# A rebuilt opening for a fused convolution and two-matmul kernel: shorter band construction, w_in in column halves, another channel order

## Chip, cores, metric

One core of a Trainium2 chip; the batches of runs went to different chips, so each run is compared with executions of the kernel before in its own rounds. The metric is the device time of one execution in microseconds (us); executions of one kernel in the same rounds lay within 0.4% of each other. In the traces PE is TensorE and PEld its weight loads, DVE is VectorE, ACT ScalarE, POOL GpSimd, SP the engine whose queue issues most of the DMAs; PSUM is the memory that matmuls write.

## The reference

x is 8 x 4096 x 192, weight 8 heads x 7 taps, w_in 192 x 2048, w_out 2048 x 192, all fp32. (Shortened:)

```python
def _attn_ref(x, weight):                       # causal convolution, one set of taps a head of 24 channels
    w = softmax(weight, axis=-1)
    x_pad = concatenate([zeros((B, 6, D)), x], axis=1)
    x_unf = x_pad[:, idx, :].reshape(B, S, K, H, group)
    return einsum('hk,bskhg->bshg', w, x_unf).reshape(B, S, D)

def _moe_ref(x, w_in, w_out):
    h = x @ w_in
    return (h * cos(h)) @ w_out
```

## The kernel before: the parts that matter

32,768 tokens are cut into 64 tiles of 512, two tiles to a unit. For each half unit the convolution is 12 matmuls on half of PE's rows (64 of 128 tokens) with band matrices as weights. Its output is transposed by DMA and feeds the first matmul (`mm1`, 192 channels as three chunks k of 64, each on an upper and a lower row half at once); then cosine on ScalarE, product on VectorE, and the second matmul (`mm2_step`).

```python
w_src = moe_w_in.rearrange("(h k r) (t f) -> k t h r f", h=H, r=R, t=2)   # channel = (head, k, r), R = 8
for k in range(NC):
    for t in range(2):
        nc.sync.dma_start(out=w_f[64 * t : 64 * t + 64, k, :, :]..., in_=w_src[k, t])     # 8 x 8 x 1024

def conv_view(ps, n):                            # where a convolution matmul writes in PSUM
    return ps[:, :, 0 : n * 2 * G].rearrange("p b (n k i r) -> p b i n k r", n=n, k=NC, i=2)

def conv_mm(u, c, pv, i, rows, prev, n0, n1, **flags):
    h = 4 * c + i
    return nc.tensor.matmul(out=pv[:, i // 2, i % 2],
        lhsT=band[rows, h, 128 if prev else 0 : 256 if prev else 128],
        rhs=bf[u][rows, n0 + 1 - prev : n1 + 1 - prev, h * G : (h + 1) * G].rearrange("p n (k r) -> p n k r", k=NC), ...)

def conv_part(u, c, ...):                        # one half unit; up = rows 0-63, lo = rows 64-127
    mm(0, up, start=True); mm(2, lo, start=True); m = mm(1, up)
    mm(2, lo, 1); mm(3, lo)
    turn.mark(m, mm(3, lo, 1))                   # ... cut
    turn.wait(mm(0, lo)); mm(0, lo, 1); mm(1, lo)
    turn.wait(mm(2, up)); mm(1, lo, 1, stop=True); mm(3, up, stop=True)
```

## Time and profile before

| | before |
|---|---|
| time, median of 4 runs | 755.75 us (755.13 to 756.02) |
| start of tile 0, 1, 2 (first mm1 matmul) | 19.6, 34.4, 52.08 us |
| from tile start to tile start, tiles 2 to 60 | 11.12 us |
| the same without convolution (last tiles) | 10.57 us |

The time of such a program is two numbers: when tile 2 starts, and the period of a tile times some 60. Two lines are needed besides those that the prediction shows. A second steady tile in the windows view (columns: start:end, length, then busy time and count on PE, weight load, DVE, ACT, POOL, then clock, DMA share, GB/s), and the group of the convolution's matmuls in the middle of the run, from 100 to 700 us (columns: out and in, shapes, count, busy us, mean ns of one, idle before):

```profile
63.16:74.28 11.12, 11.12 (x194) 9.96 (x191) 9.43 (x9) 9.66 (x13) 0.00 (x0) 1.00 0.40 123
```

```profile
L168 PE MATMUL h<-x_bf,band 64*128 64x192 bf16 x648 | 61.6, 243 | 0.0
```

The first is the regular period, 11.12; PE is busy throughout. In the second, 243 ns is how long one matmul is in the pipe. It is not its cost: successive convolution matmuls on one row half start 82 ns apart in the trace (108.408, 108.490, 108.573 us).

### The profile page before, as it was taken

How to read it: one execution, taken by the hardware profiler on the slowest of the kernel's cores; microseconds unless marked ns; L12 is line 12 of the kernel's file. 1: busy time of each engine (PE TensorE's matmuls, PEld its weight loads, DVE VectorE, ACT ScalarE, POOL GpSimd, SP SyncE). 2: the span in 40 equal slices, each digit the busy share in tenths (PEclk: the TensorE clock that was granted, in tenths of full speed). 3: DMA queues.
4: the chain of work that ended last, by engine and by line, in shares of the span. 5: the costliest groups of instructions: out<-in, count | busy, mean ns of one | idle time of the engine just before them, and what ended most of it. 6: DMA issues, size and time to landing. Idle time of an engine off the chain costs nothing.

```text
span 753.7 us, 26680 instructions
## 1 busy us (share of the span) xinstructions
PE 724.6 (96%) x12060; PEld 646.8 (86%) x12060; DVE 616.5 (82%) x533; ACT 624.4 (83%) x778; POOL 110.0 (15%) x112
## 2 busy tenths in 40 slices
PE   1699999999999999999999999999999999999997
PEld 1378999999999999999999999999999999999876
DVE  5658888888888888888888888888888888888893
ACT  3668888888888888888888888888888888888883
POOL 4310111110111110011111011111101111101000
PEclk9989999999999999999999999999999999999999
DMA  7434334334535424433432442442454543243301
GB/s 203 113 86 127 85 108 127 94 99 127 116 77 127 127 77 116 127 90 103 128 105 88 127 120 73 127 127 74 119 128 89 104 127 107 86 128 85 82 27 64
DMA packets 167633, 79.99 MB, mean 106 GB/s; under 512 B 99552, under 2 KB 167136, under 8 KB 167520
## 3 DMA queue, kind: packets, MB, share of 16 engines
q1 hardware_dynamic: 167376, 78.26, 39.1%
q8 instruction: 94, 1.54, 0.8%
q14 instruction: 19, 0.16, 0.1%
q10 hardware_dynamic: 144, 0.03, 0.0%
HBM read 28.34 MB, written 25.17 MB: 71 GB/s over the span
## 4 chain that ended last, share of the span: by engine, by line
PE 95%; POOL 1%; issue 1%; DVE 1%; ACT 1%; DMA 1%; POOLq 0%; SPq 0%
PE h L264 46%; PE o_ps L290 45%; PE h L168 3%; DMA w_bc<-in_weight_dram 1%; POOL x_bf L157 0%; POOL wo L360 0%; DVE strip L123 0%; DVE band L125 0%; ACT o_sb L302 0%; ACT cs L270 0%; DVE prod L121 0%; POOL band L125 0%; ACT w L250 0%; POOL ct L218 0%; ACT ct L182 0%
## 5 line engine op out<-in xcount | busy, mean ns | idle before, releaser
L274 DVE TENSOR_TENSOR g<-h,cs 128x1024 bf16<-128x1024 f32 x512 | 605.5, 1221 | 115.8 <-ACT cs L270 108.9
L270 ACT ACTIVATE cs<-h 128x1024 bf16<-128x1024 f32 x512 | 511.4, 1025 | 78.9 <-PE h L264 74.3
L290 PE MATMUL o_ps<-wo,g 64*128 64x192 bf16 x8192 | 452.5, 243 | 1.2 <-ACT o_sb L302 1.2
L290 PEld LDWEIGHTS <-g 64*128 64x128 bf16 x8192 | 419.8, 94 | 35.8 <-SPq L138 1.8
L264 PE MATMUL h<-cT,w 64*128 64x512 bf16 x3072 | 439.1, 379 | 2.9 <-ACT ct L182 1.3
L264 PEld LDWEIGHTS <-w 64*128 64x128 bf16 x3072 | 234.1, 94 | 37.9 <-issue 4.1
L218 POOL COPY ct<-ct 128x1536 bf16<-128x1536 bf16 (+1 forms) x32 | 46.4, 1449 | 580.9 <-ACT ct L182 580.9
L168 PE MATMUL h<-x_bf,band 64*128 64x192 bf16 (+2 forms) x784 | 74.7, 247 | 19.7 <-DVE band L125 11.4
L168 PEld LDWEIGHTS <-band 64*128 64x128 bf16 (+1 forms) x784 | 56.2, 96 | 27.6 <-DVE band L125 11.4
L182 ACT CAST ct<-h 128x384 bf16<-128x384 f32 (+1 forms) x128 | 54.4, 477 | 23.9 <-PE h L168 19.2
L302 ACT COPY o_sb<-o_ps 128x384 f32<-128x384 f32 x128 | 61.3, 479 | 10.1 <-PE o_ps L290 8.2
L157 POOL CAST x_bf<-x_f 128x1536 bf16<-128x1536 f32 (+1 forms) x32 | 46.3, 1448 | 3.1 <-DMA x_f<-in_x_dram 3.1
L156 POOL COPY x_bf<-x_bf 128x192 bf16<-128x192 bf16 x24 | 8.4, 349 | 0.0
L180 ACT CAST ct<-h 128x384 bf16<-128x384 f32 x2 | 1.0, 480 | 6.8 <-PE h L168 6.8
L121 POOL TENSOR_TENSOR prod<-mask,wn 128x1064 f32<-128x1064 f32 x1 | 3.4, 3387 | 4.6 <-DVE wn L116 4.6
L180 DVE CAST ct<-h 128x384 bf16<-128x384 f32 x2 | 1.1, 558 | 3.1 <-ACT ct L180 3.1
L109 ACT ACTIVATE wexp<-wexp 128x56 f32<-128x56 f32 x1 | 0.2, 249 | 3.4 <-DVE wexp L108 3.4
L360 POOL CAST wo<-wo_f 128x1536 bf16<-128x1536 f32 x2 | 2.9, 1469 | 0.0
L243 PE MATMUL h<-ident,ct 128*128 128x128 bf16 x12 | 1.5, 312 | 1.2 <-DVE ct L180 1.2
L123 DVE TENSOR_REDUCE strip<-prod 128x152 f32<-128x1064 f32 x2 | 2.5, 1260 | 0.1
L243 PEld LDWEIGHTS <-ct 128*128 128x128 bf16 x12 | 1.2, 144 | 1.4 <-DVE ct L180 1.4
L88 ACT ACT_TABLE_LOAD x1 | 1.3, 1283 | 1.2 <-PEq L394 1.2
(29 smaller groups left out, 18.3 us busy)
## 6 DMA issues: line engine op xcount, KB each, us to landing
out_dram<-o_sb SPq DMA_DIRECT2D x64, 384.0 KB, 2.8
x_f<-in_x_dram SPq DMA_DIRECT2D x31, 768.0 KB, 12.9
w_f<-in_moe_w_in_dram SPq DMA_DIRECT2D x6, 256.0 KB
wo_f<-in_moe_w_out_dram SPq DMA_DIRECT2D x1, 1536.0 KB
x_f<-in_x_dram SPq DMA_DIRECT2D x2, 384.0 KB, 8.9
cT<-ct SPq DMA_TRANSPOSE x32
w_bc<-in_weight_dram ACTq DMA_DIRECT2D x1, 28.0 KB, 4.8
```

Source lines behind the costliest of these rows:

```text
L121: eng.tensor_tensor(out=prod[:, hs], in0=mask.rearrange("p (o e) k -> p o e k", o=1).to_broadcast([128, 4, E, K]), in1=wn[:, hs].to_broadc ...
L156: nc.gpsimd.tensor_copy(out=bf[u][:, 0, :], in_=bf[u - 1][:, UB, :])
L157: copy(out=bf[u][:, n0 + 1 : n1 + 1, :], in_=x_tiles[u][:, n0:n1, :])
L168: return nc.tensor.matmul(out=pv[:, i // 2, i % 2], lhsT=band[rows, h, 128 if prev else 0 : 256 if prev else 128], rhs=bf[u][rows, n0 + 1 ...
L182: copies[b](o[:, :, 0, :], i[:, :, 0, :])
L218: nc.gpsimd.tensor_copy(out=ct[:, n0:n1, :, 1, :], in_=ct[:, n0:n1, :, 0, :])
L264: nc.tensor.matmul(out=h[:, i, :], lhsT=w[rows, k, j, :], rhs=c[rows, n0 : n0 + NB, k, :], start=(k == 0), stop=(k == NC - 1))
L270: nc.scalar.activation(out=cs, in_=h, func=AF.Sin, bias=math.pi / 2.0, scale=1.0)
L274: nc.vector.tensor_tensor(out=g_tiles[t][:, 2 * j : 2 * j + 2, :], in0=h, in1=cs, op=ALU.mult)
L290: m = nc.tensor.matmul(out=o_ps[tt, b][:, si * D : (si + 1) * D], lhsT=g_tiles[tt][rows, f, s * 128 : (s + 1) * 128], rhs=wo[rows, f // 2, ...
L302: nc.scalar.copy(o_sb[t][:, 2 * b : 2 * b + 2, :].rearrange("p s d -> p (s d)"), o_ps.pop((t, b))[:, 0 : 2 * D])
L360: nc.gpsimd.tensor_copy(out=wo[:, :, i, :], in_=wo_f[:, i])
```

## The change

Its intent is to start tile 0 and tile 1 sooner. The taps come as one row and are broadcast by a PE matmul; the bands are built from bf16 products of 8 taps (one of them zero) and a tree of adds on DVE alone; 19 matmuls on zeros keep PE's clock up; w_in comes in two column halves, so that tile 0 can begin on the first; unit 0's whole convolution runs ahead of tile 0. To load a column half in one DMA with 128 rows, the order of the channels within a chunk is changed too, from (head, k, r) to (row, k).

```diff
-    w_bc = consts.tile([128, H, K], FP32)       # taps to 128 rows by DMA
+    w_row = consts.tile([1, H * K], FP32)       # one row, then a PE matmul with ones
...
-    w_src = moe_w_in.rearrange("(h k r) (t f) -> k t h r f", h=H, r=R, t=2)
-    for k in range(NC):
-        for t in range(2):
-            nc.sync.dma_start(out=w_f[64 * t : 64 * t + 64, k, :, :]..., in_=w_src[k, t])
-    load_unit(0, NB, UB)
+    w_src = moe_w_in.rearrange("(m k) (t f) -> k t m f", k=NC, t=2)
+    HP = NP // 2
+    for q in range(2):
+        for k in range(NC):
+            nc.sync.dma_start(out=w_f[:, k, q * HP : (q + 1) * HP, :]...,
+                              in_=w_src[k, :, :, q * HP * 128 : (q + 1) * HP * 128])
...
+    keep_warm(3) ... keep_warm(16)              # 512-column matmuls on zeros
...
-    for eng, hs in ((nc.vector, slice(0, 4)), (nc.gpsimd, slice(4, 8))):
-        eng.tensor_tensor(out=prod[:, hs], ...)               # fp32, 7 taps
-        nc.vector.tensor_reduce(out=strip[:, hs], ...)
+    for hs in (slice(0, 4), slice(4, 8)):
+        nc.vector.tensor_tensor(out=prod[:, hs], ...)         # bf16, 8 taps
+        for m in (4, 2):
+            nc.vector.tensor_tensor(out=prod[:, hs, :, 0:m], in0=prod[:, hs, :, 0:m], in1=prod[:, hs, :, m : 2 * m], op=ALU.add)
         for q in range(4):
-            eng.tensor_copy(out=band[...], in_=strip[...])
+            nc.vector.tensor_tensor(out=band[...], in0=prod[p, hs, :, 0], in1=prod[p, hs, :, 1], op=ALU.add)
...
-        return ps[:, :, 0 : n * 2 * G].rearrange("p b (n k i r) -> p b i n k r", n=n, k=NC, i=2)
+        return ps[:, :, 0 : n * 2 * G].rearrange("p b (n k i r) -> p b i n r k", n=n, k=NC, i=2)
...
-            rhs=bf[u][...].rearrange("p n (k r) -> p n k r", k=NC),
+            rhs=bf[u][...].rearrange("p n (r k) -> p n r k", k=NC),
...
-    PE_FIRST = "h0 a1 h1 a2 b1 h2 b2 h3 | h4 h5 d1 h6 d2 c1 h7 c2 x"
+    PE_FIRST = ["h0 h1 h2 h3 h4 h5 h6 d1 h7 d2 c1 c2 |", "h0 m8 h1 m8 h2 h3 m16 | h4 c1 h5 m8 c2 h6 m12 h7 m12"]
```

(Cut: the order of casts and of w_out's loads, the masks in bf16, the generators for the opening.)

More of the change, by code (lines that the diff above doesn't have):

```diff
@@ L58 @@
     ctx.enter_context(tc.manual_schedule())
-    w_bc = consts.tile([128, H, K], FP32)
-    nc.scalar.dma_start(out=w_bc, in_=bass.AP(tensor=weight.tensor, offset=weight.offset, ap=[[0, 128], [K, H], [1, K]]))
+    w_row = consts.tile([1, H * K], FP32)
+    nc.scalar.dma_start(out=w_row, in_=weight.rearrange("(o h) k -> o (h k)", o=1))
     x_tiles = {}
@@ L72 @@
     load_unit(0, 0, NB)
+    load_unit(0, NB, UB)
     w_f = consts.tile([128, NC, NP, 128], FP32)
-    w_src = moe_w_in.rearrange("(h k r) (t f) -> k t h r f", h=H, r=R, t=2)
-    for k in range(NC):
-        for t in range(2):
-            nc.sync.dma_start(out=w_f[64 * t : 64 * t + 64, k, :, :].rearrange("p j f -> p (j f)"), in_=w_src[k, t])
-    load_unit(0, NB, UB)
+    w_src = moe_w_in.rearrange("(m k) (t f) -> k t m f", k=NC, t=2)
+    HP = NP // 2
+    for q in range(2):
+        for k in range(NC):
+            nc.sync.dma_start(out=w_f[:, k, q * HP : (q + 1) * HP, :].rearrange("p j f -> p (j f)"),
+                              in_=w_src[k, :, :, q * HP * 128 : (q + 1) * HP * 128])
@@ L80 @@
     load_unit(1)
-    wo_f = consts.tile([128, 2, NP, D], FP32)
-    nc.sync.dma_start(out=wo_f, in_=moe_w_out.rearrange("(i j p) d -> p i j d", i=2, p=128))
-    one = consts.tile([128, 1], FP32)
+    wo_f = consts.tile([128, NP, 2, D], FP32)
+    wo_src = moe_w_out.rearrange("(i j p) d -> p j i d", i=2, p=128)
+    one = consts.tile([128, 128], FP32)
     nc.vector.memset(one, 1.0)
-    scrap = consts.tile([128, 1], FP32)
-    nc.scalar.activation(out=scrap, in_=one, func=AF.Exp)
-    E = 32 + K - 1
@@ L92, with keep_warm @@
-    mask = consts.tile([128, E, K], FP32)
+    zero = consts.tile([128, T], BF16)
+    nc.vector.memset(zero, 0.0)
+    idle = o_pools[0].tile([128, T], FP32, name="o_ps0")
+    def keep_warm(n):
+        for _ in range(n):
+            nc.tensor.matmul(out=idle, lhsT=zero[:, 0:128], rhs=zero, start=True, stop=True)
+    scrap = consts.tile([128, 1], FP32)
+    nc.scalar.activation(out=scrap, in_=one[:, 0:1], func=AF.Exp)
+    keep_warm(3)
+    w_all = o_pools[1].tile([128, T], FP32, name="o_ps1")
@@ L93 @@
+    w_bc = w_all[:, 0 : H * K].rearrange("p (h k) -> p h k", k=K)
+    nc.tensor.matmul(out=w_all[:, 0 : H * K], lhsT=one[0:1, :], rhs=w_row, start=True, stop=True)
+    keep_warm(16)
+    xb0 = xbf_pool.tile([128, UB + 1, D], BF16, name="x_bf")
+    nc.gpsimd.memset(xb0[:, 0, :], 0.0)
+    E, KP = 32 + K - 1, 8
+    mask = consts.tile([128, E, KP], BF16)
     nc.gpsimd.memset(mask[0:32], 0.0)
     nc.gpsimd.affine_select(out=mask[0:32], in_=mask[0:32], compare_op=ALU.not_equal, fill=1.0, base=1 - K,
-                            pattern=[[1, E], [1, K]], channel_multiplier=-1)
+                            pattern=[[1, E], [1, KP]], channel_multiplier=-1)
@@ L96 @@
+    for q in range(1, 4):
+        nc.gpsimd.tensor_copy(out=mask[32 * q : 32 * q + 32], in_=mask[0:32])
     ident = consts.tile([128, 128], BF16)
@@ L99 @@
                             channel_multiplier=-1)
-    for q in range(1, 4):
-        nc.vector.tensor_copy(out=mask[32 * q : 32 * q + 32], in_=mask[0:32])
+    wn = consts.tile([128, H, 1, KP], BF16)
+    nc.vector.memset(wn, 0.0)
     band = consts.tile([128, H, 256], BF16)
@@ L109 @@
     nc.scalar.activation(out=wexp, in_=wexp, func=AF.Exp)
-    nc.scalar.activation(out=scrap, in_=one, func=AF.Sin)
+    nc.scalar.activation(out=scrap, in_=one[:, 0:1], func=AF.Sin)
     wsum = consts.tile([128, H, 1], FP32)
@@ L114 @@
     nc.vector.reciprocal(winv, wsum)
-    wn = consts.tile([128, H, 1, K], FP32)
-    nc.vector.tensor_tensor(out=wn[:, :, 0, :], in0=wexp, in1=winv.to_broadcast([128, H, K]), op=ALU.mult)
-    prod = consts.tile([128, H, E, K], FP32)
-    strip = consts.tile([128, H, E], FP32)
-    for eng, hs in ((nc.vector, slice(0, 4)), (nc.gpsimd, slice(4, 8))):
-        eng.tensor_tensor(out=prod[:, hs], in0=mask.rearrange("p (o e) k -> p o e k", o=1).to_broadcast([128, 4, E, K]),
-                          in1=wn[:, hs].to_broadcast([128, 4, E, K]), op=ALU.mult)
-        nc.vector.tensor_reduce(out=strip[:, hs], in_=prod[:, hs], axis=mybir.AxisListType.X, op=ALU.add)
+    nc.vector.tensor_tensor(out=wn[:, :, 0, 0:K], in0=wexp, in1=winv.to_broadcast([128, H, K]), op=ALU.mult)
+    prod = consts.tile([128, H, E, KP], BF16)
+    for hs in (slice(0, 4), slice(4, 8)):
+        nc.vector.tensor_tensor(out=prod[:, hs], in0=mask.rearrange("p (o e) k -> p o e k", o=1).to_broadcast([128, 4, E, KP]),
+                                in1=wn[:, hs].to_broadcast([128, 4, E, KP]), op=ALU.mult)
+        for m in (4, 2):
+            nc.vector.tensor_tensor(out=prod[:, hs, :, 0:m], in0=prod[:, hs, :, 0:m], in1=prod[:, hs, :, m : 2 * m], op=ALU.add)
         for q in range(4):
-            eng.tensor_copy(out=band[32 * q : 32 * q + 32, hs, 32 * q : 32 * q + E], in_=strip[32 * q : 32 * q + 32, hs])
+            p = slice(32 * q, 32 * q + 32)
+            nc.vector.tensor_tensor(out=band[p, hs, 32 * q : 32 * q + E], in0=prod[p, hs, :, 0], in1=prod[p, hs, :, 1], op=ALU.add)
     w = consts.tile([128, NC, NP, 128], BF16)
@@ L150, in cast_unit @@
         copy = nc.scalar.copy if u == 0 and n0 == 0 else nc.gpsimd.tensor_copy
-        if n0 == 0:
+        if u == 0:
+            bf[u] = xb0
+        else:
             bf[u] = xbf_pool.tile([128, UB + 1, D], BF16, name="x_bf")
@@ L170, in conv_mm @@
             lhsT=band[rows, h, 128 if prev else 0 : 256 if prev else 128],
-            rhs=bf[u][rows, n0 + 1 - prev : n1 + 1 - prev, h * G : (h + 1) * G].rearrange("p n (k r) -> p n k r", k=NC),
+            rhs=bf[u][rows, n0 + 1 - prev : n1 + 1 - prev, h * G : (h + 1) * G].rearrange("p n (r k) -> p n r k", k=NC),
             skip_group_check=True, **flags)
@@ L229, with conv_first, turn_first @@
     cast_unit(0, 0, NB)
+    cast_unit(0, NB, UB)
     ct_tiles[0] = ct_pool.tile([128, UB, NC, 2, 64], BF16, name="ct")
-    for c in range(2):
-        ps = h_pool.tile([128, 2, T], FP32, name="h")
-        for i in range(4):
-            for prev in range(2):
-                conv_mm(0, c, conv_view(ps, NB), i, slice(0, 128), prev, 0, NB, start=prev == 0 and i % 2 == 0, stop=prev == 1)
-        conv_out(0, c, ps, 0, NB, [nc.scalar.copy, nc.vector.tensor_copy], double=True)
-    cast_unit(0, NB, UB)
-    cT[0] = cT_pool.tile([128, UB, NC, 128], BF16, name="cT")
-    for half in range(2):
+    cT[0] = cT_pool.tile([128, UB, NC, 128], BF16, name="cT")
+    copies = [nc.scalar.copy, nc.vector.tensor_copy]
+    def conv_first(n0, n1):
+        for c in range(2):
+            ps = h_pool.tile([128, 2, T], FP32, name="h")
+            for i in range(4):
+                for prev in range(2):
+                    conv_mm(0, c, conv_view(ps, NB), i, slice(0, 128), prev, n0, n1,
+                            start=prev == 0 and i % 2 == 0, stop=prev == 1)
+            yield
+            conv_out(0, c, ps, n0, n1, copies, double=n0 == 0)
+    def turn_first(half):
         ps = h_pool.tile([128, 2, T], FP32, name="h")
@@ L245 @@
                                  start=True, stop=True, skip_group_check=True)
-        copy = nc.vector.tensor_copy if half else nc.scalar.copy
-        copy(out=cT[0][:, 2 * half : 2 * half + 2].rearrange("p n c k -> p n (c k)"), in_=ps[:, :, 0 : NC * 128])
-    nc.gpsimd.tensor_copy(out=w[:, 0], in_=w_f[:, 0])
-    nc.vector.tensor_copy(out=w[:, 1], in_=w_f[:, 1])
-    nc.scalar.copy(out=w[:, 2], in_=w_f[:, 2])
+        yield
+        copies[half](out=cT[0][:, 2 * half : 2 * half + 2].rearrange("p n c k -> p n (c k)"), in_=ps[:, :, 0 : NC * 128])
+    list(conv_first(0, NB))
+    b = conv_first(NB, UB)
+    next(b)
+    next(b)
+    across = [turn_first(0), turn_first(1)]
+    next(across[0])
+    list(b)
+    for half in range(2):
+        list(across[half])
+    cast = [nc.gpsimd.tensor_copy, nc.vector.tensor_copy, nc.scalar.copy]
+    for k in range(NC):
+        cast[k](out=w[:, k, 0:HP], in_=w_f[:, k, 0:HP])
+    double_unit(0, NB, UB)
+    turn_unit(0, NB, UB)
+    for q in range(2):
+        for i in range(2):
+            nc.sync.dma_start(out=wo_f[:, q * HP : (q + 1) * HP, i], in_=wo_src[:, q * HP : (q + 1) * HP, i])
+    nc.gpsimd.tensor_copy(out=w[:, :, HP:NP], in_=w_f[:, :, HP:NP])
+    cast_unit(1)
+    for q in range(2):
+        nc.gpsimd.tensor_copy(out=wo[:, q * HP : (q + 1) * HP], in_=wo_f[:, q * HP : (q + 1) * HP])
+    load_unit(2)
     g_tiles = {}
@@ L312 @@
     ACT_ORDER = "P s0 ec s1 s2 s3 Q s4 s5 s6 s7"
-    PE_FIRST = "h0 a1 h1 a2 b1 h2 b2 h3 | h4 h5 d1 h6 d2 c1 h7 c2 x"
-    ACT_FIRST = "s0 s1 ea s2 eb s3 s4 s5 s6 ed s7 ec"
+    PE_FIRST = ["h0 h1 h2 h3 h4 h5 h6 d1 h7 d2 c1 c2 |", "h0 m8 h1 m8 h2 h3 m16 | h4 c1 h5 m8 c2 h6 m12 h7 m12"]
+    ACT_FIRST = ["s0 s1 s2 s3 s4 s5 s6 ed s7 ec", "s0 s1 s2 s3 s4 s5 ec s6 s7"]
     for t in range(NT + 2):
@@ L321 @@
         if t == 0:
-            conv.update(a=conv_part(0, 0, NB, UB), b=conv_part(0, 1, NB, UB), d=conv_part(1, 0))
-        act, done, h, step = (ACT_ORDER if t else ACT_FIRST).split(), set(), {}, 0
+            conv["d"] = conv_part(1, 0)
+        act, done, h, step = (ACT_ORDER if t > 1 else ACT_FIRST[t]).split(), set(), {}, 0
         def flush():
@@ L342 @@
         flush()
-        for k in (PE_ORDER if t else PE_FIRST).split():
+        for k in (PE_ORDER if t > 1 else PE_FIRST[t]).split():
             if k[0] == "h" and t < NT:
@@ L353 @@
             flush()
-            if t == 0:
-                if k == "h3":
-                    double_unit(0, NB, UB)
-                    cast_unit(1)
-                    for i in range(2):
-                        nc.gpsimd.tensor_copy(out=wo[:, :, i, :], in_=wo_f[:, i])
-                if k == "|":
-                    turn_unit(0, NB, UB)
-                    load_unit(2)
-                if k == "x":
-                    double_unit(1)
-                    turn_unit(1)
-                    cast_unit(2)
-                continue
+            if k == ("|" if t == 0 else "h1") and second == 0 and cu < NU:
+                double_unit(cu)
             if k == "|":
@@ L377 @@
                     cast_unit(u + 2)
-            if k == "h1" and second == 0 and cu < NU:
-                double_unit(cu)
 _INS = ['x', 'weight', 'moe_w_in', 'moe_w_out']
```

## The prediction

> **What bounds the kernel now.** I read the page first, then the windows, then the chain of waits of the first 45 us, then the waits of the same stretch. The page's busy rows:
>
> ```profile
> PE 724.6 (96%) x12060; PEld 646.8 (86%) x12060; DVE 616.5 (82%) x533; ACT 624.4 (83%) x778; POOL 110.0 (15%) x112
> ...
> PE   1699999999999999999999999999999999999997
> ...
> PE h L264 46%; PE o_ps L290 45%; PE h L168 3%; DMA w_bc<-in_weight_dram 1%; POOL x_bf L157 0%; POOL wo L360 0%; DVE strip L123 0%; DVE band L125 0%; ACT o_sb L302 0%; ACT cs L270 0%; DVE prod L121 0%; POOL band L125 0%; ACT w L250 0%; POOL ct L218 0%; ACT ct L182 0%
> ```
>
> Slices are 18.8 us: PE is idle in the first, part idle in the second, full from there to the end. So only two things can move the time: when PE gets to its steady tiles, and how long one steady tile is. The stretches in the windows view (columns: PE, weight load, DVE, ACT, POOL busy with counts, then clock, DMA share, GB/s):
>
> ```profile
> 12.20:14.30 2.10, 0.00 (x0) 0.00 (x0) 0.48 (x1) 0.00 (x0) 1.37 (x5) 1.00 0.50 186
> ...
> 39.40:44.70 5.30, 5.23 (x40) 3.98 (x41) 0.61 (x1) 1.89 (x3) 0.02 (x1) 0.50 0.56 127
> 52.08:63.16 11.08, 11.08 (x193) 9.04 (x190) 9.50 (x9) 9.71 (x13) 3.17 (x3) 1.00 0.37 89
> 718.87:729.44 10.57, 10.57 (x179) 8.05 (x176) 9.52 (x8) 8.91 (x11) 0.00 (x0) 1.00 0.12 40
> ```
>
> Tile 2 begins at 52.08; a tile with its half unit of convolution takes 11.08 us, one without 10.57. The convolution (12 half-array matmuls of 192 columns) costs 0.51 us a tile, as near to free as it can be. Before tile 2, the chain:
>
> ```profile
> 0.74 4.85 DMA w_bc<-in_weight_dram
> ...
> 8.43 1.27 DVE strip L123
> ...
> 14.17 0.27 POOL x_bf L154
> ...
> 19.61 1.54 PE h L264 x6
> ...
> 38.01 1.42 POOL x_bf L157
> ```
>
> Taps, bands, transposes; tile 0 starts at 19.6; tile 1 waits 4.1 us for POOL's cast of unit 2 until 39.5, and then runs at half clock until 44.7 (third fence). Taking one 11.08 us tile off 52.08, tile 1 starts in effect at 41.0. That is the number the change must beat.
>
> **What the Trainium skill says.** (1) "DMA: Bandwidth & Descriptors", section "Why a DMA increments its semaphore by 16 and not by 1": a load runs on the largest k of at most 16 engines that divides the slowest dimension, not of size 1, of both its patterns, always the lowest-numbered ones. This case agrees: a w_in load has 8 x 8 x 1024 at the source, and in 12.2 to 14.3 us, where little but w_in is moving, the DMA share is 0.50; the trace's semaphore events have 8 landings for each w_in load and 16 for each x load. (2) "PSUM — Partial Sum Buffer", "Specifications (TRN2)": lines of 8 bytes, and a pattern that isn't contiguous slows matmuls. No run here shows it yet: all matmuls of before write runs of at least 8 fp32. (3) "TensorE: Matmul & The Clock Gate", Part 1: an idle PE falls to half clock and needs some 3.4 us of work to recover. Agrees: 0.50 in the row above after the wait of 4.1 us. (4) "VectorE: DVE Perf Modes", "The perf-mode tier table": bf16 tensor_tensor in SBUF at two elements a cycle, reductions at one. The fp32 product of 1064 takes 1.27 us here, the reduction 1.26.
>
> **The change part by part.**
> Taps: 56 numbers in one row instead of 128 rows, spread by one PE matmul. w_bc landed at 5.6; the row should land near 3.2, the matmul end near 3.6: 2 us sooner. Softmax steps stay (wmax to wn 1.5 us): wn at 5.1.
> Bands: for half the heads before 1.27 + 1.26 + 1.67 on DVE, the rest on POOL with waits, all done at 14.1. Now per half: a product of 1216 at two a cycle 0.8, adds of 608 and 304 some 0.5 and 0.3, four band adds of 152 at 0.23: 2.5 us. Both halves done at 5.1 + 5.0 = 10.1: 4 us sooner.
> Convolution, copies, transposes for tile 0: convolution to 10.7, copies to 11.8 (0.49 ACT, 0.56 DVE), transposes and the cT copies (0.80, 0.96) to about 14. Tile 0 could start at 14.4 instead of 19.6 if w_in is there. Then eight steps at DVE's 1.2 us, with unit 1's convolution behind, would put tile 1 at about 25.7, and without the 4.1 us wait, since c1 moves behind h4. That is the intent: 41.0 - 25.7 = 15 us, 740.6 in all.
>
> w_in is what I don't believe. Its new source pattern is 2 x 64 x 512 (the two row halves outermost), the target 128 rows. By (1) k is 2, where it was 8. One engine moves 186/8 = 23 GB/s by the window above, up to 26 from single packets (4096 bytes in 159 ns). Two give about 48 GB/s: 262,144 bytes take 5.4 us, and six loads in a row on the same two engines 32.4. Behind unit 0's x they start at 5.1 (before, the first w_in packet came at 3.9 after one x load; one more x load is 1.2): the third lands at 5.1 + 16.2 + 0.9 = 22.2, the sixth at 38.4. (Before, all six had landed by 16.8.)
> - Tile 0: ACT casts the third part (1.05 us for 1024, 0.55 for 512), so h0 starts at 22.8, 3.2 us later than before. h0 to h3 use the first column half. h4 waits for POOL's cast of the second half: 38.4 + 1.47 = 39.9.
> - Unit 1's x, unit 0's second transpose and w_out have shares on the same two engines, hence land at 41, 43 and 44 to 48.
> - h4 to h6 run cold at 1.5 us (as 1.54 at 19.61 before) to 44.3; then d1, h7 (after g5), d2, c1, c2; ACT's ed comes ahead of s7. Tile 1 starts at 48, loses 0.8 waiting for g7, and finds w_out just cast. Tile 2 starts at 48 + 0.8 + 11.0 = 59.8: 7.7 us later than before.
> Sum of the opening with k = 2: 755.9 + 7.7 = 763.6.
>
> Convolution of every unit: the channel order changes from (head, k, r) to (row, k), so a convolution matmul now writes PSUM in order n, r, k with k 16 fp32 apart: no two successive columns are neighbours, where there were runs of 8. If by (2) each column then takes a line to itself and the rate halves, 192 columns at full clock go from 80 to 160 ns; six pairs a tile add 0.48 us, and PE is 100% busy in those tiles, so nothing hides it. 60 tiles from tile 1 on carry convolution: 60 x 0.48 = 29 us. The opening runs mostly cold and hardly feels it. Sum: 763.6 + 29 = 792.6.
>
> keep_warm: 19 matmuls of 512 columns end near 10.5, in time for the convolution, but PE would go cold again waiting for w_in, so they are worth under 0.5 us.
>
> **Rivals.**
> A: the intent works (the load is spread after all, strides in PSUM are free): 741. For it: the windows show nothing against the shorter bands, and the parts look tuned to one another. Against: 8 landings for an outermost 8. 8%.
> B: two engines, but strides in PSUM are free: 764. For it: no trace here shows the penalty. 25%.
> C: both: 793. 50%.
> D: two engines and a part of the penalty (only first writes or only accumulations): some 777. 10%.
> E: load spread, penalty in full: 741 + 29 = 770. 7%.
>
> **Range and chances.** C and B hold most of it, C more, as the page states the line size without reserve and the first-principle number fits a PE at two columns per line. I put the time at 787, a little under C for the weight below it, and 757 to 799 as the range that holds B, D, E and C. Faster by over 2% needs A with luck: 0.06. Within 2% (740.8 to 771.0) is B, most of E and half of A: 0.34. Slower: 0.60.
>
> **What would show it.** Right on the load: DMA share near 0.12 and under 60 GB/s between 10 and 35 us, w_in's second half landing near 38, PE idle from about 29 to 40 with h4 after POOL's cast, tile 2 at about 60. Wrong: a share of 0.5 or 1 there, tile 0 at 14 to 15 and tile 2 near 37. Right on PSUM: a tile with convolution at about 11.56 in the middle of the run, tiles without it still 10.57; wrong: 11.08 as before. The bands should be done near 10 in either case; if they aren't, DVE's bf16 products don't run at two a cycle.

## More of the kernel before

All runs told here were fast: the granted clock of the whole span lay between 0.98 and 1.00.

Count by row half: four matmuls on `up`, eight on `lo`, because only the last tokens of the previous block, which lie in the lower rows, contribute to the next one (`prev` = 1).

## The result, and the profile after

The time after is 800.71 us (median of 4, 800.47 to 800.91) against 755.75: ratio 1.0596, 95% interval 1.0578 to 1.0614, slower. Ratios here and below are worked out from the fast runs of the same rounds by the program that timed them, so they are not quite the ratio of the medians quoted. The result is correct.

| | before | predicted | after |
|---|---|---|---|
| taps normalised | 7.1 | 5.1 | 4.9 us |
| bands done | 14.1 | 10.1 | 13.0 us |
| third, sixth w_in load landed | all by 16.8 | 22.2, 38.4 | 21.2, 37.3 us |
| h4 starts | | 39.9 | 38.9 us |
| tile 1, tile 2 start | 34.4, 52.08 | 48, 59.8 | 46.6, 58.8 us |
| period of a tile with convolution | 11.12 | 11.56 | 11.77 us |

The page's busy rows of the kernel after (slices of 20 us), and the chain that ended last, by line:

```profile
PE 772.0 (97%) x12073; PEld 676.3 (85%) x12073; DVE 619.0 (77%) x541; ACT 624.1 (78%) x776; POOL 107.8 (13%) x111
...
PE   6299999999999999999999999999999999999997
...
PE h L313 44%; PE o_ps L339 42%; PE h L191 8%; DMA w_f<-in_moe_w_in_dram 2%; SPq L80 2%; DVE g L323 1%; ACT cs L319 0%; POOL w L295 0%; ACT o_sb L351 0%; ACT ct L205 0%; SPq L69 0%; SPq L159 0%
```

PE now has a hole in the second slice, and the convolution (line 191) has grown from 3% of the chain to 8%. The windows, the same columns as before:

```profile
12.20:14.30 2.10, 1.26 (x11) 1.27 (x12) 1.33 (x3) 0.15 (x1) 0.00 (x0) 0.81 0.13 51
26.40:38.90 12.50, 0.00 (x0) 0.00 (x1) 2.20 (x2) 0.99 (x1) 1.52 (x2) 0.50 0.72 112
70.77:82.54 11.77, 11.77 (x193) 10.56 (x191) 9.44 (x9) 9.66 (x13) 0.00 (x0) 1.00 0.42 124
764.20:774.80 10.60, 10.60 (x180) 8.06 (x176) 9.55 (x9) 8.94 (x11) 0.00 (x0) 1.00 0.13 41
```

First row: w_in alone is moving, at a share of 0.13, two of 16 engines, where before the same stretch had 0.50. (0.50 was eight engines; each w_in load now has 2 landings in the trace's events, before 8.) Second row: PE stands still for 12.5 us. Third and fourth: a tile with convolution costs 11.77 us, PE full, one without still 10.60. The chain of waits of the opening says who held PE:

```profile
7.47 5.00 SPq L80
...
17.58 19.74 DMA w_f<-in_moe_w_in_dram
...
37.38 1.48 POOL w L295
...
38.90 4.02 PE h L313 x13
```

Columns: start, length, what. w_in's transfers run until 37.32, POOL casts the second half, PE goes on at 38.90. The last three issues on line 80 last 5 us each as well: the queue itself was held up, so that everything behind w_in left late. And the convolution's group between 100 and 700 us:

```profile
L191 PE MATMUL h<-x_bf,band 64*128 64x192 bf16 x612 | 91.1, 352 | 0.0
```

243 ns in the pipe became 352; successive starts on one row half went from 82 to 163 ns (106.924, 107.088, 107.251 us).

The sum: tile 2 starts 58.82 - 52.08 = 6.7 us later, and 59 tiles cost 11.77 - 11.12 = 0.65 us more each, 38.4 us. Together 45.1; the spans (799.1 and 753.7) differ by 45.4. Six sevenths of the loss is in the steady state, which a change called an opening was not meant to touch.

### The profile page after: what moved, and what is told of

It reads as the page before. It is cut to its first block, busy times and chain, and to the rows that moved or that the text cites. A ratio compares the mean times of both kernels' runs of the same rounds, so it can differ in the third digit from the quotient of the medians.

```text
span 799.1 us, 26715 instructions
## 1 busy us (share of the span) xinstructions
PE 772.0 (97%) x12073; PEld 676.3 (85%) x12073; DVE 619.0 (77%) x541; ACT 624.1 (78%) x776; POOL 107.8 (13%) x111
## 4 chain that ended last, share of the span: by engine, by line
PE 93%; DMA 2%; SPq 2%; ACT 1%; DVE 1%; POOL 0%; issue 0%
PE h L313 44%; PE o_ps L339 42%; PE h L191 8%; DMA w_f<-in_moe_w_in_dram 2%; SPq L80 2%; DVE g L323 1%; ACT cs L319 0%; POOL w L295 0%; ACT o_sb L351 0%; ACT ct L205 0%; SPq L69 0%; SPq L159 0%
## 5 line engine op out<-in xcount | busy, mean ns | idle before, releaser
L313 PE MATMUL h<-cT,w 64*128 64x512 bf16 x3072 | 476.7, 381 | 16.6 <-POOL w L295 12.6
L339 PE MATMUL o_ps<-wo,g 64*128 64x192 bf16 x8192 | 486.0, 243 | 1.2 <-ACT o_sb L351 1.2
L339 PEld LDWEIGHTS <-g 64*128 64x128 bf16 x8192 | 437.8, 95 | 36.2 <-SPq L159 1.8
L313 PEld LDWEIGHTS <-w 64*128 64x128 bf16 x3072 | 244.4, 98 | 66.1 <-issue 21.0
L191 PE MATMUL h<-x_bf,band 64*128 64x192 bf16 (+1 forms) x776 | 115.5, 355 | 3.7 <-DVE band L146 3.6
L191 PEld LDWEIGHTS <-band 64*128 64x128 bf16 (+1 forms) x776 | 70.6, 111 | 10.6 <-DVE band L146 4.3
L95 PE MATMUL o_ps<-zero 128*128 128x512 bf16 x19 | 6.7, 521 | 1.3 <-DVE zero L90 1.3
L95 PEld LDWEIGHTS <-zero 128*128 128x128 bf16 x19 | 2.2, 123 | 4.6 <-issue 2.5
L146 DVE TENSOR_TENSOR band<-prod 32x152 bf16<-32x152 bf16 x8 | 3.7, 466 | 0.1
L143 DVE TENSOR_TENSOR prod<-prod 128x608 bf16<-128x608 bf16 (+1 forms) x4 | 2.3, 582 | 0.1
```

Of the source, the lines that this page charges most:

```text
L95: nc.tensor.matmul(out=idle, lhsT=zero[:, 0:128], rhs=zero, start=True, stop=True)
L191: return nc.tensor.matmul(out=pv[:, i // 2, i % 2], lhsT=band[rows, h, 128 if prev else 0 : 256 if prev else 128], rhs=bf[u][rows, n0 + 1 ...
L313: nc.tensor.matmul(out=h[:, i, :], lhsT=w[rows, k, j, :], rhs=c[rows, n0 : n0 + NB, k, :], start=(k == 0), stop=(k == NC - 1))
L339: m = nc.tensor.matmul(out=o_ps[tt, b][:, si * D : (si + 1) * D], lhsT=g_tiles[tt][rows, f, s * 128 : (s + 1) * 128], rhs=wo[rows, f // 2, ...
```

## The experiments

Theories at the start. **T1**: w_in runs on two DMA engines because the row halves (2) are the outermost dimension at its source. **T2**: a convolution matmul with no two neighbouring columns in PSUM runs at half its rate. **T3**: what that costs a tile is set by the row half with more of those matmuls, eight of 163 - 82 ns. Rivals: the load is slow for another reason (short rows, one queue); the time is lost in x's strided read and not in PSUM; matmuls of the two halves cost as six pairs, with something else adding the rest. The edits are against the kernel after if not said otherwise.

### fan16: the loads alone mended

```diff
-            nc.sync.dma_start(out=w_f[:, k, q * HP : (q + 1) * HP, :]..., in_=w_src[k, :, :, ...])
+            for t in range(2):
+                nc.sync.dma_start(out=w_f[64 * t : 64 * t + 64, k, q * HP : (q + 1) * HP, :]..., in_=w_src[k, t, :, ...])
```

Twelve loads of 64 rows in place of six of 2 x 64; the strides in PSUM stay.

> The changed kernel with one edit: each w_in load is split by row half, so that the slowest dimension of its source is 64, not 2; everything else, the strided PSUM writes too, stays. Theory (two engines were the opening's loss): 16 landings for each load, w_in all landed by about 11 us, tile 0 at 16 to 17, tile 2 at about 38 instead of 58.8, so 800.7 - 21 = 780; tile period unchanged at 11.77. Rival (the opening is held by its new order of PE, POOL or w_out and not by the load): tile 2 stays past 50 and the time above 790.

Measured: 785.95 us, before in the same rounds 754.63, ratio 1.0409 (1.0393 to 1.0425), correct. Window 6 to 10 us:

```profile
6.00:10.00 4.00, 3.50 (x18) 1.50 (x17) 3.86 (x7) 0.42 (x1) 1.46 (x2) 1.00 0.98 249
```

All 16 engines, 249 GB/s. Tile 2 starts at 42.62, the period is still 11.77. T1 holds: the same bytes in rows of the same length on the same queue, with the halves taken apart, give 14.8 us back (800.71 - 785.95, across two batches), which leaves the rival of short rows or of one queue no room. It was 6 us more than I expected, as tile 0 did not start at 16 to 17 but at 18.29: the bands are late (see below), not w_in, of which the last part landed at 12.1.

### runs8: loads mended and the old channel order

```diff
-    w_src = moe_w_in.rearrange("(m k) (t f) -> k t m f", k=NC, t=2)
+    w_src = moe_w_in.rearrange("(h k r) (t f) -> k t h r f", h=H, r=R, t=2)      # loads split by t as in fan16
-    ... "p b (n k i r) -> p b i n r k"      and      "p n (r k) -> p n r k"
+    ... "p b (n k i r) -> p b i n k r"      and      "p n (k r) -> p n k r"
```

> The changed kernel with the old channel order (head, k, r), hence PSUM runs of 8 fp32, and the w_in loads split by row half (8 x 8 x 512 at the source, 8 engines), still in two column halves. Theory (k = 2 and PSUM strides are the whole loss): tile period back to 11.12, tile 2 at about 39, time 755.75 - 13 = 743, faster than before by 1.7%. Rival (something else in the new opening costs too): tile 2 at 45 or later, 750 or more.

Measured: 745.98 us, ratio 0.9884 (0.9867 to 0.9900), correct: some 55 us faster than the kernel after, and faster than the one before by 1.2%, though the interval leaves out 1. Tile 2 starts at 41.92, 3 us later than expected, and the time is 3 us above the 743 expected, again with the bands first in the chain; the period is 11.12.

```profile
6.00:10.00 4.00, 2.65 (x18) 1.15 (x16) 3.86 (x7) 0.45 (x2) 1.11 (x2) 1.00 0.53 180
```

Eight engines (share 0.53) are enough here. From fan16 to runs8 only the channel order and the number of engines change; the period falls by 0.65 and the time by 40.0.

### bstride: the channel order alone, put into the kernel before

```diff
# against before
-    w_src = moe_w_in.rearrange("(h k r) (t f) -> k t h r f", h=H, r=R, t=2)
+    w_src = moe_w_in.rearrange("(m k) (t f) -> k t m f", k=NC, t=2)
-    "p b (n k i r) -> p b i n k r",  "p n (k r) -> p n k r"
+    "p b (n k i r) -> p b i n r k",  "p n (r k) -> p n r k"
```

> The kernel before with the changed kernel's channel order alone (row, k), hence PSUM columns 16 fp32 apart; w_in loads stay split by row half (64 x 1024 at the source, 16 engines). Theory (strides cost the same 0.65 us a tile whatever the opening): period 11.77, 60 tiles, so 755.75 + 39 = 795 less up to 2 us for w_in on 16 engines. Rival (the longer period comes from something else in the changed program): 752 to 757.

Measured: 795.14 us against 754.63, ratio 1.0536 (1.0519 to 1.0552), correct; tile 2 at 54.28 and period 11.77. Nothing else of the change is in this kernel, and its w_in goes over 16 engines: the order of channels by itself costs 0.65 us a tile, plus 2.2 us in the opening (1.2 of them in the first 15 matmuls of the convolution in the chain: 2.57 us, before 1.37).

```profile
L168 PE MATMUL h<-x_bf,band 64*128 64x192 bf16 x612 | 91.2, 352 | 0.0
```

### noprev: four matmuls of the lower row half left out (wrong)

```diff
-        mm(2, lo, 1)
         mm(3, lo)
-        turn.mark(m, mm(3, lo, 1))
+        # ... and likewise without mm(0, lo, 1), mm(1, lo, 1): four on each half are left
```

> Wrong result on purpose: the changed kernel without the four matmuls of the previous block (all on the lower row half) in each half unit of convolution from unit 1 on. Of the 12 convolution matmuls 8 were on the lower half and 4 on the upper; now 4 and 4. Theory of lanes (the two row halves are two lanes, the period is set by the lower one, each strided matmul takes 163 ns in its lane): 11.77 - 4 x 0.163 = 11.12. Theory of pairs, as in the prediction (12 matmuls are six pairs): 11.77 - 2 x 0.163 = 11.44.

Measured: 761.66 us (two runs), ratio 1.0091 (1.0069 to 1.0113), period 11.113; a steady tile:

```profile
69.62:80.73 11.11, 11.11 (x189) 8.68 (x186) 9.43 (x9) 9.67 (x13) 0.00 (x0) 1.00 0.44 129
```

Four matmuls less take 0.65 us off the tile, 4 x 0.163. Pairs would have given 11.44, lanes 11.12. T3 holds for the strided kernel.

### pairs, singles, pairs_odd: how short may a run in PSUM be?

All three are runs8 (old channel order, mended loads) with only the target of the convolution matmul changed (in pairs_odd ACT's copy reads one fp32 further too), and the wrong results that follow; x is read as before, in runs of 8. Two runs each.

```diff
# pairs: runs of 2 fp32, beginning on 8 bytes
+    "p b (n k i a e) -> p b i a (n k) e", e=2
# singles: runs of 1
+    "p b (n k i r) -> p b i r (n k)"
# pairs_odd: as pairs, all of it one fp32 further, so that each run straddles an 8-byte border
+    ps[:, :, 1 : 1 + n * 2 * G]...
```

> Wrong result on purpose (columns land in permuted places): the kernel of run runs8 with every convolution matmul writing PSUM in runs of two fp32 that share an 8-byte line, then a jump of 16 fp32. Theory (a matmul writes one 8-byte line at a time, two neighbours cost what one does): full rate, tile period 11.12, time within 1 us of 746. Rival (any break in the run slows it, or the jump does): about 11.77 and 785.

> Wrong result on purpose, the control of run pairs: the same kernel with runs of one fp32, jump of 16. Both theories: period 11.77, about 785, as in run fan16. If it is 11.12, the slow writes of the changed kernel come from its runs of three (k innermost) and not from single columns.

> Wrong result on purpose: as run pairs, but all PSUM places of the convolution one fp32 further, so that each run of two straddles an 8-byte border. Theory of aligned 8-byte lines: both columns of a pair take a line each, so 11.77 and 785. Rival (what counts is that two neighbours follow each other, wherever they lie): 11.12 and 746.

| run | us | ratio | period |
|---|---|---|---|
| pairs | 745.61 | 0.9880 | 11.12 |
| singles | 784.58 | 1.0396 | 11.76 |
| pairs_odd | 785.60 | 1.0410 | 11.76 |

The convolution's group between 100 and 700 us, in this order:

```profile
L192 PE MATMUL h<-x_bf,band 64*128 64x192 bf16 x636 | 60.4, 243 | 0.0
```

```profile
L192 PE MATMUL h<-x_bf,band 64*128 64x192 bf16 x612 | 90.9, 351 | 0.0
```

```profile
L192 PE MATMUL h<-x_bf,band 64*128 64x192 bf16 x612 | 90.8, 351 | 0.0
```

It is the write to PSUM and not the read of x. Runs of two fp32 cost nothing if they begin on 8 bytes; the same runs moved by 4 bytes cost as much as single elements. What fits all of these runs is a rate set by lines of 8 bytes, one a step; "contiguous or not" is too coarse, as the aligned pairs and the runs of 8 have jumps between them as well.

### runs8_cold and runs8_cold_again: without the zeros; runs8_again; runs8_whole: without column halves

```diff
# cold: runs8 without keep_warm(3) and keep_warm(16)
# whole: runs8 with six loads of 1024 columns, the casts taking all of w[:, k], no second cast on POOL
```

> The kernel of run runs8 without its 19 matmuls on zeros, to price that part. Theory of the author (a warm PE shortens the opening): the 24 convolution matmuls at 13 us take about 3.6 us as in the cold profile of the changed kernel instead of 2.1, transposes some 0.3 longer: tile 2 at 43.5 to 44.5, 748. My prediction's claim (worth under 0.5 us): 746.0 to 746.5.

Measured: 745.07 against 754.83, ratio 0.9872; runs8 in another batch had 0.9884. The difference was within the noise, so runs8 and this kernel were sent together, with the third:

> The kernel of run runs8 once more, beside the next two on one chip, to compare within a microsecond: 745 to 746.5, tile 2 at 41.9.

> The kernel of run runs8_cold once more. Its first profile had tile 2 at 41.38, 0.5 us before run runs8, as the taps' matmul no longer waits behind three matmuls on zeros, and the convolution met a cold PE without loss, since DVE's band adds hold it. If that is so: 0.3 to 1 us under runs8_again. If the difference was one of chips or rounds: equal or above.

> The kernel of run runs8 with w_in loaded and cast in whole columns (six loads of 1024 columns, one cast on each of POOL, DVE and ACT), to price the column halves. Theory (the halves let tile 0 start earlier): six loads land by 15 to 17, casts of 1.05 on ACT after that, h0 0.5 to 1.5 us later, 746 to 747.5. Rival (DVE's bands and cT copy set the start of tile 0, w_in is in time either way): within 0.5 us of runs8_again.

| run (same rounds, before 755.51) | us | ratio, 95% | tile 0, tile 2 start |
|---|---|---|---|
| runs8_again | 745.47 | 0.9865 (0.9850 to 0.9880) | 17.27, 41.60 |
| runs8_cold_again | 745.40 | 0.9863 (0.9848 to 0.9877) | 16.90, 41.42 |
| runs8_whole | 746.09 | 0.9878 (0.9861 to 0.9894) | 17.65, 41.90 |

The zeros are worth nothing. The chain of runs8, then that of runs8_cold:

```profile
2.79 0.62 PE o_ps L103 x2
...
12.95 2.10 PE h L192 x24
```

```profile
2.07 0.66 PE o_ps L102 x2
...
12.28 2.10 PE h L190 x24
```

In both, the last 24 convolution matmuls before tile 0 take 2.10 us once DVE's bands are done. The traces show why the zeros don't help. The matmul that spreads the taps (first line of each fence) stands behind the first three zeros on PE and starts 0.72 us later, and the bands are 0.67 us later with it. And the zeros in runs8 end at 8.1 us: the granted clock was 0.65 from 12 to 14 us and 0.50 from 14 to 16, when the convolution ran. In runs8_again it fell only at 13.6; the late bands remain, and tile 0 starts 0.37 us after that of runs8_cold_again. The expectation for runs8_cold_again, 0.3 to 1 us less than runs8_again, did not come true (0.07). The column halves gave 0.6 us by the medians, and the intervals overlap: not separable.

### noprev_before: the same four matmuls left out of the kernel before (wrong)

> Wrong result on purpose: the kernel before without the four previous-block matmuls of each half unit, all on the lower row half. Lanes: each costs 192 columns = 0.0815 us in the lower lane, 11.12 - 4 x 0.0815 = 10.79. Pairs: 11.12 - 2 x 0.0815 = 10.96.

Measured: 750.59 against 755.51, ratio 0.9931; period 11.04, a steady tile:

```profile
63.12:74.16 11.04, 10.97 (x190) 8.39 (x187) 9.51 (x9) 9.67 (x13) 0.00 (x0) 1.00 0.39 121
```

A miss for both theories: lanes expected 10.79, pairs 10.96. Without stride, four matmuls less save 0.08 us. PE shows 0.07 us of gaps, and no engine listed is full. The timeline of the same tile, from 63.1 to 74.2 us, has what the lanes wait for, DVE's product of the tile's first step and PE's third step h2:

```profile
65.04 1.22 DVE L270 TENSOR_TENSOR g<-h,cs 128x1024 bf16<-128x1024 f32 x1 [0.41 <-ACT cs L266]
...
66.31 1.47 PE L260 MATMUL h<-cT,w 64*128 64x512 bf16 x12
```

The first matmuls' results and the convolution's take turns in three PSUM buffers (`h_pool`), so that h2 gets the buffer of h0 and can't start before the product has read it: 65.04 + 1.22 = 66.26, and h2 starts at 66.31. In this run h2 starts 0.05 us after that product's end in all of the tiles 10 to 57, and in the ten tiles between 100 and 211 us both row halves stand idle for 0.23 to 0.26 us before it: 10.79 + 0.25 = 11.04. So the lanes' sum holds here too, with one wait for a buffer on top. In noprev h2 starts 0.12 us after the product, in the kernel after 0.49, so this wait doesn't bind there and the verdict on noprev stands; in the kernel before it is 0.05 again, so there the full lower half and the buffer meet. All this is read from the traces; no run changed the buffers.

## Why the prediction was wrong, point by point

The prediction put 787.0 with a range to 799, and the time was 800.7. Its main rival, C (two engines and strides both cost), was the right one; of its two terms one was right, one too small.

**The opening, +7.7: right.** Measured +6.7. The load on two engines, its landings at 22.2 and 38.4, POOL's cast as the last wait, h4 at 39.9 and tile 2 at 59.8 are each there within 1.4 us, all a little sooner. fan16 shows the cause: taken apart by row half, the loads go over 16 engines and tile 2 starts 16.2 us sooner.

**"Six pairs a tile add 0.48 us": this step failed.** That a matmul goes from 80 to 160 ns was right (82 to 163). Wrong was how many of them count. The prediction took the 12 half-array matmuls as six pairs, as if every one on the upper rows had one on the lower beside it. The code has four and eight. The halves run beside each other, each at its own pace, and the longer one sets the tile: 8 x 0.0815 = 0.65 us. This is what the period shows (11.77 - 11.12), in bstride as well, and what noprev undoes by evening the halves out. The sum of the lower half's own work says the same to 0.01 us: in the traces mm1's matmuls start 216 ns apart on one half (24 in a tile), mm2's 82.5 (64 in a tile), together 10.46 us; with eight convolution matmuls of 82.5 ns that is 11.12, with eight of 163 ns 11.76, with four of 163 ns 11.11, and the periods measured are 11.12, 11.77 and 11.11.

That six pairs of 80 ns (0.48) lie close to the 0.51 that the prediction read for the convolution is chance. The 0.51 came from one window of 11.08 and from 10.57; the regular difference is 0.55, and the tile without convolution is itself not full, 10.57 us for 10.46 of work on a half.

Over the run, 59 x 0.65 = 38.4 in place of 29: 9.4 of the 13.7 us between 787.0 and 800.7. The rest is the lowering from C's 792.6 to 787.0 for the weight of the rivals (5.6), and the opening's 1.0 the other way; 0.3 are left of roundings. With the right count the same sum would have said 755.9 + 7.7 + 38.4 = 802.

**Rivals.** A (741) and B (764) fall with fan16, singles and bstride. D (a part of the penalty) falls too: first writes and accumulations both run at half rate, since four fewer accumulations in noprev save the full 4 x 0.163, and the whole 0.65 of a tile needs all eight. E (770) is fan16, which took 785.95, for E had both the small term and an opening worth 15 us. In fan16 the opening gained 52.08 - 42.62 = 9.5 us and in runs8 52.08 - 41.92 = 10.2.

**Bands done at 10.1: wrong by 2.9 us, hidden in this kernel.** w_in came later anyway; in runs8 the bands hold tile 0. The timeline of the kernel after from 5 to 13 us, of which the rows of DVE and POOL (start, busy, engine, line, what, count):

```profile
5.03 0.79 DVE L140 TENSOR_TENSOR prod<-mask,wn 128x1216 bf16<-128x1216 bf16 x1
5.54 0.97 POOL L180 CAST x_bf<-x_f 128x768 bf16<-128x768 f32 x1 [1.41 <-DMA x_f<-in_x_dram]
5.86 1.46 DVE L143 TENSOR_TENSOR prod<-prod 128x608 bf16<-128x608 bf16 x2
7.35 1.72 DVE L146 TENSOR_TENSOR band<-prod 32x152 bf16<-32x152 bf16 x4
9.10 0.79 DVE L140 TENSOR_TENSOR prod<-mask,wn 128x1216 bf16<-128x1216 bf16 x1
...
9.93 0.94 DVE L143 TENSOR_TENSOR prod<-prod 128x608 bf16<-128x608 bf16 x2
10.81 0.62 POOL L289 CAST w<-w_f 128x512 bf16<-128x512 f32 x1 [4.30 <-DMA w_f<-in_moe_w_in_dram]
10.90 2.08 DVE L146 TENSOR_TENSOR band<-prod 32x152 bf16<-32x152 bf16 x4
```

The product takes 0.79, where 0.8 was predicted. Undisturbed, the adds of a half take 0.94 together, where 0.8 was predicted, and the four band adds 1.72, where 4 x 0.23 = 0.92 was: that is the larger error, some 0.8 us a half. (0.23 is what a contiguous fp32 to bf16 copy of the same size took before; the band adds read one bf16 in each 16 bytes.) The rest is overlap with POOL: where a cast of POOL runs, the adds take 1.46 and the band adds 2.08, 0.5 and 0.4 more. The Trainium skill, "SBUF — State Buffer", section "Who interferes with whom", says that a DVE instruction with two inputs in SBUF contends with a GpSimd instruction that reads SBUF. The rows agree with it, and so does runs8_cold: there POOL's casts run at 5.95 and 7.25 us, and the long band adds move with them (0.93 from 6.15 and 0.74 from 7.52, where the others take 0.41 to 0.43). Both half sums with the two overlaps: 2 x (0.79 + 0.94 + 1.72) + 0.5 + 0.4 = 7.8 from 5.03 on, some 12.8, and PE begins at 13.0. That the step of 16 bytes makes the band adds slow fits the numbers; no run tested it. The prediction's own sign for this, that late bands would mean products not at two elements a cycle, pointed at the wrong part: the product came out on time and the bands were late.

**keep_warm worth under 0.5 us: right** (0.07 apart, in the direction of no zeros). **"The opening runs mostly cold and hardly feels it" (the stride): wrong, though hidden in the kernel after, where PE waits for w_in.** bstride lost 2.2 us in the opening, and in fan16 the 24 convolution matmuls before tile 0 took 2.89 us, in runs8 2.10.

## What to carry to other kernels

Before a layout is chosen for the sake of one load, look at what it does to the innermost two elements of every matmul's output in PSUM: a gain of 10 us once is easily paid with 0.65 us in each of 60 tiles. Where matmuls share the array by row halves, count them for each half by itself; the longer count sets the time, not the number of pairs. And look at the outermost dimension on both sides of a transfer before it is merged with another: a load of 2 x 64 rows ran on two DMA engines, where two loads of 64 rows ran on 16.

## What the Trainium skill lacked or had wrong

- "PSUM — Partial Sum Buffer", "Specifications (TRN2)", and "Advanced Engine Details and Errata", "PSUM Cachelines": they say that a pattern which isn't contiguous slows matmuls significantly, and give no size. Here it is a factor of two: 82 to 163 ns between starts of 192-column matmuls. The second page adds that every two consecutive elements should be contiguous; what it lacks is that the pair must also begin on 8 bytes: aligned pairs 243 ns in the pipe and 11.12 us a tile, the same pairs shifted by one fp32 351 ns and 11.76, as slow as single elements. And "any" is too wide on both pages: the aligned pairs and the runs of 8 aren't contiguous from end to end and run at the full rate.
- "TensorEngine Tiling (Array Packing)", "Key Properties": tiles operate independently. This agrees, and the page lacks the consequence: with four matmuls on one row half and eight on the other, the eight set the time (0.65 us, where pairs would give 0.48).
- "TensorE: Matmul & The Clock Gate", Part 1: the stretch at half clock after a wait agrees (0.50 from 26.4 to 38.9). What it lacks is what a warm-up on zeros can cost: here the taps' matmul behind the first three started 0.72 us later, and the whole brought nothing (745.47 us with, 745.40 without).
